# Retention and token-mixing kernel on one core: the q loads of batches 2 and 3 issued from the scalar engine, and 15 instead of 24 zero matmuls at the start

## The chip, the core and the metric

The kernel runs on one core of one Trainium2 chip. The number that counts is the device time of one execution in microseconds, as the median of several executions. Engines are called by the names of the profile: PE is TensorE's matmul, PEld its weight load, DVE is VectorE, ACT is ScalarE, POOL is GpSimd, SP is SyncE. SP computes nothing here: it issues the DMAs.

## The reference: what is computed

Inputs are q, k and v of shape (batch 4, heads 8, sequence 768, head size 64) and three weight matrices, all float32. The first half is a decaying linear attention, written as a recurrence over the sequence:

```
state = gamma[h] * state + outer(k[t], v[t])
y[t]  = q[t] @ state / sqrt(64)
```

The heads of y are laid side by side to x of shape (4, 768, 512). The second half mixes tokens:

```
wq, wk = x @ w_q, x @ w_k
mixed  = (wq @ wk.T / sqrt(64)) @ x
out    = relu(mixed) @ w_out
```

The output has the shape (4, 768, 512) in float32.

## The kernel before, in words

The sequence of a batch is cut into six chunks of 128 tokens, and two chunks make a pair, so there are 12 pairs, numbered p = 0 to 11, three to a batch: pairs 0 to 2 are batch 0, pairs 9 to 11 are batch 3. The recurrence is done chunk by chunk: scores inside a chunk, masked, times v, plus q times the state that the chunks before left. The decay is folded into k by a table (fk, fk2) and into the result by another (gx).

The kernel is written as a list of short tokens, ORDER (lines 18 to 68). Each engine issues its own instructions in the order in which the tokens stand there. A token has a name, a pair, sometimes PSUM banks after "@", and after ":" the engine that does it (A is ACT, V is DVE, P is POOL). These matter here:

- ck, cq, cv cast k, q and v of a pair from their staging buffer to bf16 (function cast, from line 391); trk, trq transpose k and q on PE, ekT, eqT bring the transposed tiles out of PSUM.
- sc makes the scores of a chunk, eat masks them, st adds a chunk to the state in PSUM, es copies the state out (es.5.0:A is the copy for pair 5, chunk 0, on ACT), in and ia make the two parts of y, ex scales it.
- xt, exN, wqk, ew, za, zm, ez, mx, r, pj, eo are the second half. pj is the output projection, and eo copies its result out of PSUM and issues the store (line 770).
- warmup issues matmuls of a zero tile (line 374), fill issues a few more between the first real ones.

Loads. All loads of batches 0 and 1, and the weights, are issued at the start from SP in the order of LOADS (line 77), pair by pair, 512 KB each. Batches 2 and 3 come into the same staging buffers, which batches 0 and 1 have left: a load may go out once the cast that read the buffer is done. In the kernel before these loads are issued from inside cast. After the cast of q of pair p (p below 6) come the two loads of 256 KB for q of pair p+6 (load_pair, lines 204 to 223). After the last cast of k or v of a batch comes one load of 1.5 MB for the whole of k or v two batches on (load, line 202). In what follows k2B, v2B, k3B and v3B are these four loads for batches 2 and 3. q6 to q11 are the q loads of pairs 6 to 11, each in two halves a and b.

Since all these DMAs are issued from SP, they go out in the order of the tokens: q6, q7, k2B, q8, v2B, q9, k3B, q10, q11, v3B, and then the 24 stores. The framework puts in all the waits. It gives each DMA one of eight semaphores, in turn, which the DMA raises when it has landed.

Of the kernel before, what the change touches and what calls it, by code (L numbers as in the profile page):

```python
# [15 lines left out]


ORDER = """
warmup.24 cv.0:A ck.0:V trk.0@4 ekT.0:V cq.0:P fill.3 trq.0@5
eqT.0:V fill.5 sc.0.0@0+1 sc.0.1@2+3 st.0.0 es.0.0:A in.0.1@4 eat.0.0:V  # L20
ia.0.0@5 eat.0.1:V ia.0.1 st.0.1 ck.1:P trk.1@6 cq.1:A es.0.1:A
ekT.1:A ck.2:P ex.0.0:V ex.0.1:V trq.1@2 eqT.1:V fill.1 sc.1.0@0+1
# [7 lines left out]
za.0@4 zm.0 sc.3.1@0+1 ck.4:P WO:A ck.5:P cv.4:P st.3.1  # L30
ez.0:V mx.1@4+5 mx.0@6+2 r.1.1:A r.0.0:A r.0.1:A eat.3.1:V cq.4:V
in.3.1@5 trk.4@6 trq.4@2 r.1.0:V pj.1.1@4 ekT.4:V es.3.1:V eqT.4:A
ia.3.0@6 sc.4.0@0+1 ia.3.1 pj.0.1@2 cq.5:P cv.5:P cq.7:P eo.1.1:A
eo.0.1:A pj.0.0@4 eat.4.0:V ex.3.1:V ex.3.0:V mx.2@5+2 st.4.0 cq.6:P
trk.5@6 r.2.1:V sc.4.1@0+1 trq.5@2 es.4.0:V eqT.5:V r.2.0:A eo.0.0:A
ekT.5:A st.4.1 in.4.0@4 wqk.3@5 in.4.1@6 eat.4.1:V ia.4.0 sc.5.0@2+3
ia.4.1 ew.3:V es.4.1:A sc.5.1@0+1 st.5.0 es.5.0:A pj.2.0@5 eo.2.0:A
ex.4.0:V eat.5.0:V ex.4.1:V pj.2.1@4 in.5.0@5 in.5.1@2 trq.6@6 eo.2.1:A
eqT.6:A pj.1.0@4 ia.5.0 eat.5.1:V ia.5.1 ex.5.1:V ex.5.0:V xt.3@6
eo.1.0:A xt.4@4 exN.4:V wqk.4@2 xt.5@5 ew.4:V exN.5:V exN.3:A  # L40
wqk.5@6 ck.6:P cq.8:A trk.6@4 ew.5:A trq.8@2 zm.1@5 ekT.6:V
eqT.8:V sc.6.1@0+1 trq.7@4 ck.7:P trk.7@6 ez.1:A mx.4@5+2 eat.6.1:V
sc.6.0@0+1 ck.8:P eqT.7:A r.4.0:A ekT.7:V mx.3@4+6 trk.8@5 r.4.1:A
sc.7.1@2+3 r.3.1:A r.3.0:A eat.6.0:V sc.7.0@0+1 pj.4.0@6 ekT.8:A pj.3.0@4
eo.4.0:A eat.7.1:V eat.7.0:V cv.6:P st.6.0 sc.8.1@2+3 sc.8.0@0+1 es.6.0:A
st.6.1 eo.3.0:A ia.6.0@5+6 ia.6.1 cv.8:P cv.7:P in.6.1 es.6.1:A
st.7.0 eat.8.1:V es.7.0:A cq.9:P pj.3.1@4 ex.6.0:V ex.6.1:V in.7.0@5+2
st.7.1 ia.7.0 ia.7.1 eo.3.1:A in.7.1 eat.8.0:V ex.7.0:V es.7.1:A
in.8.0@4+6 st.8.0 ia.8.1 es.8.0:A ia.8.0 in.8.1 ex.7.1:V trq.9@5
ex.8.1:V ex.8.0:V wqk.7@2 xt.7@6 exN.7:V ew.7:V eqT.9:A xt.6@5  # L50
xt.8@4 exN.6:V ck.9:P trk.9@6 wqk.8@2 cq.10:A exN.8:A trq.10@5
ekT.9:V mx.5@4+6 sc.9.1@0+1 ew.8:A sc.9.0@2+3 eqT.10:V ck.10:P trk.10@5
r.5.1:A r.5.0:A eat.9.1:V eat.9.0:V ekT.10:A ck.11:P cq.11:A wqk.6@6
pj.4.1@4 eo.4.1:V sc.10.0@0+1 sc.10.1@2+3 trk.11@5 trq.11@4 ew.6:A pj.5.1@6
ekT.11:A eat.10.1:V eqT.11:V eat.10.0:V zm.2@5 cv.9:P st.9.0 eo.5.1:A
ia.9.0@4+6 ia.9.1 es.9.0:A in.9.1 st.9.1 ez.2:V mx.6@5+2 es.9.1:A
sc.11.1@0+1 r.6.1:A cv.10:P st.10.0 es.10.0:A ex.9.1:V pj.5.0@6 r.6.0:A
st.10.1 eat.11.1:V eo.5.0:A mx.7@5+2 sc.11.0@0+1 ex.9.0:V es.10.1:A r.7.1:A
cv.11:P in.10.0@6+4 in.10.1 ia.10.0 st.11.0 ia.10.1 pj.6.0@2 eat.11.0:V
r.7.0:A ex.10.1:V ex.10.0:V in.11.0@4+5 es.11.0:A in.11.1 ia.11.0 ia.11.1  # L60
ex.11.1:V ex.11.0:V eo.6.0:A pj.7.1@6 xt.10@5 eo.7.1:V wqk.10@2 wqk.9@4
ew.9:V ew.10:A exN.10:A xt.11@6 exN.11:V xt.9@2 exN.9:V wqk.11@4
ew.11:A pj.6.1@5 za.3@4 zm.3 mx.8@6+2 eo.6.1:A ez.3:A r.8.0:A
r.8.1:V pj.7.0@5 pj.8.1@4 mx.9@6+2 eo.7.0:A r.9.0:A r.9.1:V eo.8.1:A
pj.8.0@5 eo.8.0:V pj.9.0@6 mx.10@4+5 eo.9.0:V r.10.1:A pj.9.1@2 mx.11@5+6
eo.9.1:A r.10.0:V pj.10.0@4 eo.10.0:V pj.10.1@2 eo.10.1:V r.11.1:A r.11.0:A
pj.11.0@5 eo.11.0:V pj.11.1@4 eo.11.1:A
""".split()


SPLIT = (0, 1)


BY_PAIR = ("q2", "q3")
# [9 lines left out]
def kernel(  # L84
# [19 lines left out]
    nc = tc.nc  # L104
# [25 lines left out]
    def buf(name, i, shape, dtype):  # L130

        if (name, i) not in made:
            made[name, i] = const(f"{name}{i}", shape, dtype)
        return made[name, i]
# [25 lines left out]
    def copy(e, out, in_):  # L160
        if e == "A":
            nc.scalar.copy(out=out, in_=in_)  # L162
        else:
            ENGINES[e].tensor_copy(out=out, in_=in_)  # L164
# [4 lines left out]
    def split(p):  # L169
        return p // NP in SPLIT  # L170
# [11 lines left out]
    def whole(name, b):  # L182
        return name != "q" and b not in SPLIT

    def raw(name, b):
        if (name, b) not in staged:
            staged[name, b] = buf(name + "_st", b % 2, [H * NCH * D], FP32)
        return staged[name, b]

    def stage(name, b):  # L190

        order = "n h e" if b in SPLIT or f"{name}{b}" in BY_PAIR else "h n e"
        return raw(name, b).rearrange(
            f"p ({order}) -> p n h e", n=NCH if whole(name, b) else NP, h=H
        )

    def load(name, b):
        if whole(name, b):
            n, src = NCH, SRC[name][b].rearrange("h (n p) d -> p (h n) d", p=128)
        else:  # L200
            n, src = NP, SRC[name][b].rearrange("h (n p j) d -> p (h n) (j d)", p=128, j=2)
        nc.sync.dma_start(out=raw(name, b).rearrange("p (m e) -> p m e", m=H * n), in_=src)

    def load_pair(name, p):
        b, n = divmod(p, NP)
        src = SRC[name][b, :, n * 2 * C : (n + 1) * 2 * C, :]
        if whole(name, b):
            for c in range(2):
                nc.sync.dma_start(
                    out=stage(name, b)[:, 2 * n + c],  # L210
                    in_=src[:, c * C : (c + 1) * C, :].rearrange("h p d -> p h d"),
                )
        elif split(p):
            nc.sync.dma_start(  # L214
                out=stage(name, b)[:, n], in_=src.rearrange("h (p j) d -> p h (j d)", j=2)
            )
        else:

            for o in range(2):
                nc.sync.dma_start(  # L220
                    out=stage(name, b)[:, n, o * HP : (o + 1) * HP],
                    in_=src.rearrange("(m o) (p j) d -> o p m (j d)", o=2, j=2)[o],
                )
# [6 lines left out]
    for part in LOADS:  # L230
        if part == "W":
            nc.sync.dma_start(out=wq_stage, in_=moe_w_q.rearrange("(a p) h -> p a h", p=128))  # L232
            nc.sync.dma_start(out=wk_stage, in_=moe_w_k.rearrange("(a p) h -> p a h", p=128))  # L233
        elif part == "WO":
            nc.sync.dma_start(out=wout_stage, in_=moe_w_out.rearrange("(a p) m -> p a m", p=128))  # L235
        elif part[0] in SRC:
            load_pair(part[0], int(part[1:]))
        else:
            load(part[0].lower(), int(part[1:]))
# [8 lines left out]
    def temp(i):  # L248

        return buf("o0_", 2, [DM], FP32)[:, i * 64 : i * 64 + NCH * H]  # L250
# [22 lines left out]
    lq = temp(3).rearrange("p (n j h) -> p n j h", n=NP, j=2)  # L273
# [60 lines left out]
    for t, base in ((cmask2, 0), (cmask2_b, C)):  # L334
        nc.gpsimd.memset(t, 1.0)
        for j in range(2):
# [4 lines left out]
                fill=0.0,  # L341
# [49 lines left out]
    def cast(e, name, p, table):  # L391
        st = pairs[p]
        b, cp = divmod(p, NP)
        t = buf(name + "s", p % N_CAST, [2, H, D], BF16)
        st[name + "s"] = t
        if whole(name, b):
            in_ = stage(name, b)[:, 2 * cp : 2 * cp + 2]
        else:
            in_ = stage(name, b)[:, cp].rearrange("p h (j d) -> p j h d", j=2)
        if table is None:  # L400
            copy(e, t, in_)
        elif split(p):
            ENGINES[e].tensor_tensor(  # L403
                out=t, in0=in_, in1=table.to_broadcast([128, 2, H, D]), op=ALU.mult
            )
        else:

            for j in range(2):
                ENGINES[e].tensor_tensor(  # L409
                    out=t[:, j].rearrange("p (o m) d -> p o m d", o=2),  # L410
                    in0=in_[:, j].rearrange("p (m o) d -> p o m d", o=2),
                    in1=table[:, j]
                    .rearrange("p (m o) -> p o m", o=2)[:, :, :, None]
                    .to_broadcast([128, 2, HP, D]),
                    op=ALU.mult,
                )
        casts[name, b] = casts.get((name, b), 0) + 1

        if b + 2 in SPLIT or f"{name}{b + 2}" in BY_PAIR:
            load_pair(name, p + 2 * NP)  # L420
        elif casts[name, b] == NP and b + 2 < B:
            load(name, b + 2)

    def ck(e, at, p):
        cp = p % NP
        cast(e, "k", p, fk2[:, cp] if split(p) else fk[:, 2 * cp : 2 * cp + 2])

    def cq(e, at, p):
        cast(e, "q", p, None)

    def cv(e, at, p):
        cast(e, "v", p, None)
# [331 lines left out]
    def eo(e, at, p, j):  # L764
# [8 lines left out]
        "ck": ck, "cq": cq, "cv": cv, "trk": trk, "ekT": ekT, "trq": trq, "eqT": eqT, "sc": sc,  # L773
        "eat": eat, "msk": msk, "st": st_, "es": es, "in": in_, "ia": ia, "ex": ex, "xt": xt,
        "exN": exN, "wqk": wqk, "ew": ew, "za": za, "zm": zm, "ez": ez, "mx": mx, "r": r,
        "pj": pj, "eo": eo, "W": W, "WO": WO, "fill": fill, "warmup": warmup,
    }

    for token in ORDER:
        token, _, e = token.partition(":")  # L780
        token, _, at = token.partition("@")
# [33 lines left out]
```

## Time and profile before

| | |
|---|---|
| time, median of 3 | 103.28 us (103.1 to 104.06) |
| span of the profiled execution | 102.8 us |
| PE busy | 87.8 us, 85% |
| PEld busy | 61.1 us, 59% |
| DVE busy | 76.6 us, 75% |
| ACT busy | 60.8 us, 59% |
| POOL busy | 40.2 us, 39% |
| DMA | 26.71 MB, mean 260 GB/s |
| granted TensorE clock | 1.0 over the span |

The profile is of one execution. Its views name an instruction by line, engine, operation and the tiles that it writes and reads. A line of a timeline gives the start and the length in us, then the instruction, then in square brackets the idle time of the engine before it and what ended it. "SPq" marks a DMA issue on SP; its length is the time that the issue took on SP, not the time in which the data moved. A line of waits gives the total, the number and the longest of a kind of wait, in us. A line of windows gives a stretch of the execution, for each engine its busy time in the stretch with the number of instructions, and at its end the granted clock, the busy share of the DMA engines and the GB/s.

### The profile page before, as it was taken

Reading aid. Unit: us, or ns where it says so; the run is one execution under the profiler, and the core shown is the slowest. Engines: PE = TensorE matmul, PEld = TensorE weight load, DVE = VectorE, ACT = ScalarE, POOL = GpSimd, SP = SyncE. Lnnn points to the kernel's source line nnn. Section 1 sums busy time; section 2 is a strip of 40 time slices with the busy share of each in tenths; the row PEclk is TensorE's granted clock in tenths of the full one; section 3 lists DMA queues with packets and bytes.
Section 4 is the critical chain, followed back from the end, with each engine's and each line's share of the span. In section 5 each row is a group of like instructions: output and inputs, shape, how many; then the busy total and the mean of one; then the engine's idle time right before and its main releaser. Section 6 shows DMA issues by size and latency. Waiting matters only on the chain.

```text
span 102.8 us, 3767 instructions
## 1 busy us (share of the span) xinstructions
PE 87.8 (85%) x1607; PEld 61.1 (59%) x1617; DVE 76.6 (75%) x124; ACT 60.8 (59%) x104; POOL 40.2 (39%) x51
## 2 busy tenths in 40 slices
PE   5999668597976989999899789958999999999950
PEld 1347557486864748868776357847665669533410
DVE  5845777989989597995888699855998976248440
ACT  6784664228689638367549454339967825564620
POOL 6843654900024296705980690399055000000000
PEclk9999999999999999999999999999999999999999
DMA  1999999999988999967992699999799932036663
GB/s 25 303 347 347 347 343 245 267 305 367 341 240 255 341 336 303 331 195 204 267 305 59 196 262 326 270 276 293 242 406 403 380 134 105 4 131 233 247 263 145
DMA packets 36320, 26.71 MB, mean 260 GB/s; under 512 B 2000, under 2 KB 32720, under 8 KB 36304
## 3 DMA queue, kind: packets, MB, share of 16 engines
q1 hardware_dynamic: 36304, 26.48, 82.6%
q8 instruction: 12, 0.20, 0.7%
q14 instruction: 4, 0.03, 0.1%
HBM read 20.19 MB, written 6.29 MB: 257 GB/s over the span
## 4 chain that ended last, share of the span: by engine, by line
SPq 34%; PE 32%; issue 12%; POOL 10%; DMA 5%; ACT 2%; DVE 1%; POOLq 0%; ACTq 0%
SPq L214 25%; PE bank_ps L755 11%; POOL ks L409 6%; DMA q_st<-in_q_dram 5%; SPq L220 3%; POOL vs L164 3%; PE duo_ps L755 3%; PE bank_ps L441 2%; SPq L235 2%; PE bank_ps L734 2%; PE bank_ps L598 2%; PE bank_ps L651 2%; SPq L233 2%; PE bank_ps L553 2%; SPq L232 2%
## 5 line engine op out<-in xcount | busy, mean ns | idle before, releaser
L755 PE MATMUL bank_ps<-wout_sb,relu 128*128 128x512 bf16 x72 | 18.9, 380 | 0.6 <-issue 0.3
L162 ACT CAST s_sb<-bank_ps 64x256 bf16<-64x256 f32 (+1 forms) x26 | 9.6, 370 | 14.9 <-PE bank_ps L598 14.8
L509 DVE TENSOR_TENSOR at<-duo_ps,cmask 128x1024 bf16<-128x1024 f32 x12 | 14.5, 1220 | 2.2 <-PE duo_ps L486 2.2
L638 DVE TENSOR_TENSOR xT<-bank_ps,gx 128x512 bf16<-128x512 f32 x22 | 14.4, 685 | 2.3 <-PE bank_ps L571 1.0
L502 DVE TENSOR_TENSOR at<-duo_ps,cmask 128x1024 bf16<-128x1024 f32 x12 | 14.5, 1218 | 2.0 <-PE duo_ps L475 2.0
L409 POOL TENSOR_TENSOR ks<-k_st,fk 128x512 bf16<-128x512 f32 x12 | 12.2, 1048 | 8.0 <-PE bank_ps L651 4.4
L164 POOL CAST vs<-v_st 128x1024 bf16<-128x1024 f32 x10 | 10.2, 1038 | 10.3 <-DMA v_st<-in_v_dram 10.3
L403 POOL TENSOR_TENSOR ks<-k_st,fk 128x1024 bf16<-128x1024 f32 x4 | 7.6, 1903 | 16.0 <-PE bank_ps L708 9.5
L755 PEld LDWEIGHTS <-relu 128*128 128x128 bf16 x96 | 8.2, 98 | 8.9 <-issue 0.6
L162 ACT COPY o<-bank_ps 128x512 f32<-128x512 f32 x14 | 8.2, 586 | 4.4 <-PE bank_ps L755 4.4
L747 ACT ACTIVATE relu<-bank_ps 128x512 bf16<-128x512 f32 x15 | 8.6, 603 | 2.5 <-PE bank_ps L734 1.1
L162 ACT CAST qs<-q_st 128x1024 bf16<-128x1024 f32 x6 | 6.3, 1046 | 3.6 <-DMA q_st<-in_q_dram 3.6
L598 PE MATMUL bank_ps<-vs,ks 64*64 64x64 bf16 (+1 forms) x240 | 7.5, 195 | 1.1 <-POOL vs L164 1.1
L376 PE MATMUL bank_ps<-warm 128*128 128x512 bf16 x24 | 7.0, 465 | 1.2 <-DVE warm L246 1.2
L598 PEld LDWEIGHTS <-ks 64*64 64x64 bf16 (+1 forms) x240 | 6.0, 109 | 3.1 <-issue 1.9
L441 PE MATMUL bank_ps<-identity,ks 128*128 128x128 bf16 x88 | 7.0, 220 | 0.8 <-POOL ks L409 0.6
L164 DVE COPY kT<-bank_ps 128x1024 bf16<-128x1024 bf16 x6 | 4.1, 688 | 4.0 <-PE bank_ps L441 4.0
L441 PEld LDWEIGHTS <-ks 128*128 128x128 bf16 x96 | 5.6, 98 | 2.4 <-POOL ks L409 1.0
L475 PE MATMUL duo_ps<-qT,kT 64*64 64x128 bf16 x192 | 4.6, 219 | 2.9 <-DVE qT L164 1.1
L441 PEld LDWEIGHTS <-qs 128*128 128x128 bf16 x96 | 5.8, 98 | 1.5 <-ACT qs L162 1.2
L164 POOL CAST qs<-q_st 128x1024 bf16<-128x1024 f32 x5 | 5.1, 1039 | 3.0 <-DMA q_st<-in_q_dram 3.0
L651 PEld LDWEIGHTS <-xT 128*128 128x128 bf16 x96 | 5.7, 98 | 0.5 <-issue 0.2
(98 smaller groups left out, 167.4 us busy)
## 6 DMA issues: line engine op xcount, KB each, us to landing
out_dram<-o SPq DMA_DIRECT2D x24, 256.0 KB, 2.8
k_st<-in_k_dram SPq DMA_DIRECT2D x6, 512.0 KB, 6.0
q_st<-in_q_dram SPq DMA_DIRECT2D x6, 512.0 KB, 6.2
v_st<-in_v_dram SPq DMA_DIRECT2D x6, 512.0 KB, 7.0
q_st<-in_q_dram SPq DMA_DIRECT2D x12, 256.0 KB, 4.9
wout_stage<-in_moe_w_out_dram SPq DMA_DIRECT2D x1, 1024.0 KB, 9.6
o<-in_moe_w_q_dram SPq DMA_DIRECT2D x1, 128.0 KB, 6.2
o<-in_moe_w_k_dram SPq DMA_DIRECT2D x1, 128.0 KB, 5.0
```

The costliest lines, as they stand in the source:

```text
L162: nc.scalar.copy(out=out, in_=in_)
L164: ENGINES[e].tensor_copy(out=out, in_=in_)
L214: nc.sync.dma_start(out=stage(name, b)[:, n], in_=src.rearrange("h (p j) d -> p h (j d)", j=2))
L409: ENGINES[e].tensor_tensor(out=t[:, j].rearrange("p (o m) d -> p o m d", o=2), in0=in_[:, j].rearrange("p (m o) d -> p o m d", o=2), in1=t ...
L441: nc.tensor.transpose(ps[:, i, hp, :] if whole(name, p // NP) else slots[:, :, hp, i, :], pairs[p][name + "s"][:, i, 2 * hp : 2 * hp + 2, ...
L502: nc.vector.tensor_tensor(out=t.rearrange("p x (hi j) t -> p (x hi) (j t)", j=2), in0=ps.rearrange("p x (hi j) t -> p (x hi) (j t)", j=2), ...
L509: nc.vector.tensor_tensor(out=t.rearrange("p x hp t -> p (x hp) t"), in0=ps.rearrange("p x hp t -> p (x hp) t"), in1=cmask.rearrange("p o ...
L598: nc.tensor.matmul(out=state_ps[rows(x), m, :], lhsT=st["ks"][ps, slot, 2 * m + x, :], rhs=st["vs"][ps, slot, head(p, m, x), :], start=(n ...
L638: nc.vector.tensor_tensor(out=st["xT", i], in0=st["y", i], in1=table, op=ALU.mult)
L651: nc.tensor.transpose(ps[:, c, a, :], xT(p, a, c), identity)
L747: nc.scalar.activation(out=dst, in_=st["mx"][half], func=ACT.Relu)
L755: nc.tensor.matmul(out=ps, lhsT=st["relu", a // 2][:, a % 2, j], rhs=wout_sb[:, a, :], start=(a == 0), stop=(a == NDM - 1),)
```

## The change

Two things are changed. First, the q loads of batches 2 and 3 are no longer issued from SP by cast. They have tokens of their own, lq.6 to lq.11, which issue the two halves from ACT's DMA queue at a place in ACT's order that ORDER sets. SP then has only k2B, v2B, k3B, v3B and the stores left after the loads of the start. This is to keep the small q loads from standing behind the large k and v loads, and the large ones behind them. Second, 15 zero matmuls instead of 24 stand ahead of the first transposes on PE. They keep PE busy until the first k has come. The rest of ORDER keeps its sequence; some PSUM banks around pairs 6 to 8 are others.

```diff
-warmup.24 cv.0:A ck.0:V trk.0@4 ekT.0:V cq.0:P fill.3 trq.0@5
+warmup.15 cv.0:A ck.0:V trk.0@4 ekT.0:V cq.0:P fill.3 trq.0@5
...
+ia.3.0@6 sc.4.0@0+1 ia.3.1 pj.0.1@2 cq.5:P cv.5:P lq.6:A lq.7:A
+cq.7:P eo.1.1:A eo.0.1:A pj.0.0@4 eat.4.0:V ex.3.1:V ex.3.0:V mx.2@5+2
...
+ia.4.0 sc.5.0@2+3 ia.4.1 ew.3:V es.4.1:A sc.5.1@0+1 st.5.0 lq.8:A
+es.5.0:A pj.2.0@5 eo.2.0:A ex.4.0:V eat.5.0:V ex.4.1:V pj.2.1@4 in.5.0@5
+in.5.1@2 trq.6@6 eo.2.1:A lq.9:A eqT.6:A pj.1.0@4 ia.5.0 eat.5.1:V
+ia.5.1 ex.5.1:V ex.5.0:V xt.3@6 eo.1.0:A xt.4@4 exN.4:V wqk.4@2
+xt.5@5 ew.4:V exN.5:V exN.3:A wqk.5@6 ck.6:P lq.10:A cq.8:A
+trk.6@4 ew.5:A trq.8@5 zm.1@6 ekT.6:V eqT.8:V sc.6.1@0+1 trq.7@4
+ck.7:P trk.7@5 ez.1:A mx.4@6+2 eat.6.1:V sc.6.0@0+1 ck.8:P lq.11:A
+eqT.7:A r.4.0:A ekT.7:V mx.3@4+5 trk.8@6 r.4.1:A sc.7.1@2+3 r.3.1:A
...
-    def load_pair(name, p):
+    def load_pair(name, p, queue=nc.sync):
...
-                nc.sync.dma_start(
+                queue.dma_start(
...
-        if b + 2 in SPLIT or f"{name}{b + 2}" in BY_PAIR:
+        if name == "q":
+            pass
+        elif b + 2 in SPLIT or f"{name}{b + 2}" in BY_PAIR:
             load_pair(name, p + 2 * NP)
         elif casts[name, b] == NP and b + 2 < B:
             load(name, b + 2)
+
+    def lq_(e, at, p):
+
+        load_pair("q", p, nc.scalar)
```

More of the change, by code (lines that the diff above doesn't have):

```diff
@@ L32 @@
 in.3.1@5 trk.4@6 trq.4@2 r.1.0:V pj.1.1@4 ekT.4:V es.3.1:V eqT.4:A
[L33 to L67, printed above, removed]
+ia.3.0@6 sc.4.0@0+1 ia.3.1 pj.0.1@2 cq.5:P cv.5:P lq.6:A lq.7:A
+cq.7:P eo.1.1:A eo.0.1:A pj.0.0@4 eat.4.0:V ex.3.1:V ex.3.0:V mx.2@5+2
+st.4.0 cq.6:P trk.5@6 r.2.1:V sc.4.1@0+1 trq.5@2 es.4.0:V eqT.5:V
@@ new lines @@
+r.2.0:A eo.0.0:A ekT.5:A st.4.1 in.4.0@4 wqk.3@5 in.4.1@6 eat.4.1:V
+ia.4.0 sc.5.0@2+3 ia.4.1 ew.3:V es.4.1:A sc.5.1@0+1 st.5.0 lq.8:A
[5 more added lines that the diff above has]
+ck.7:P trk.7@5 ez.1:A mx.4@6+2 eat.6.1:V sc.6.0@0+1 ck.8:P lq.11:A
@@ new lines @@
+eqT.7:A r.4.0:A ekT.7:V mx.3@4+5 trk.8@6 r.4.1:A sc.7.1@2+3 r.3.1:A
+r.3.0:A eat.6.0:V sc.7.0@0+1 pj.4.0@5 ekT.8:A pj.3.0@4 eo.4.0:A eat.7.1:V
+eat.7.0:V cv.6:P st.6.0 sc.8.1@2+3 sc.8.0@0+1 es.6.0:A st.6.1 eo.3.0:A
+ia.6.0@5+6 ia.6.1 cv.8:P cv.7:P in.6.1 es.6.1:A st.7.0 eat.8.1:V
+es.7.0:A cq.9:P pj.3.1@4 ex.6.0:V ex.6.1:V in.7.0@5+2 st.7.1 ia.7.0
+ia.7.1 eo.3.1:A in.7.1 eat.8.0:V ex.7.0:V es.7.1:A in.8.0@4+6 st.8.0
+ia.8.1 es.8.0:A ia.8.0 in.8.1 ex.7.1:V trq.9@5 ex.8.1:V ex.8.0:V
+wqk.7@2 xt.7@6 exN.7:V ew.7:V eqT.9:A xt.6@5 xt.8@4 exN.6:V
@@ new lines @@
+ck.9:P trk.9@6 wqk.8@2 cq.10:A exN.8:A trq.10@5 ekT.9:V mx.5@4+6
+sc.9.1@0+1 ew.8:A sc.9.0@2+3 eqT.10:V ck.10:P trk.10@5 r.5.1:A r.5.0:A
+eat.9.1:V eat.9.0:V ekT.10:A ck.11:P cq.11:A wqk.6@6 pj.4.1@4 eo.4.1:V
+sc.10.0@0+1 sc.10.1@2+3 trk.11@5 trq.11@4 ew.6:A pj.5.1@6 ekT.11:A eat.10.1:V
+eqT.11:V eat.10.0:V zm.2@5 cv.9:P st.9.0 eo.5.1:A ia.9.0@4+6 ia.9.1
+es.9.0:A in.9.1 st.9.1 ez.2:V mx.6@5+2 es.9.1:A sc.11.1@0+1 r.6.1:A
+cv.10:P st.10.0 es.10.0:A ex.9.1:V pj.5.0@6 r.6.0:A st.10.1 eat.11.1:V
+eo.5.0:A mx.7@5+2 sc.11.0@0+1 ex.9.0:V es.10.1:A r.7.1:A cv.11:P in.10.0@6+4
@@ new lines @@
+in.10.1 ia.10.0 st.11.0 ia.10.1 pj.6.0@2 eat.11.0:V r.7.0:A ex.10.1:V
+ex.10.0:V in.11.0@4+5 es.11.0:A in.11.1 ia.11.0 ia.11.1 ex.11.1:V ex.11.0:V
+eo.6.0:A pj.7.1@6 xt.10@5 eo.7.1:V wqk.10@2 wqk.9@4 ew.9:V ew.10:A
+exN.10:A xt.11@6 exN.11:V xt.9@2 exN.9:V wqk.11@4 ew.11:A pj.6.1@5
+za.3@4 zm.3 mx.8@6+2 eo.6.1:A ez.3:A r.8.0:A r.8.1:V pj.7.0@5
+pj.8.1@4 mx.9@6+2 eo.7.0:A r.9.0:A r.9.1:V eo.8.1:A pj.8.0@5 eo.8.0:V
+pj.9.0@6 mx.10@4+5 eo.9.0:V r.10.1:A pj.9.1@2 mx.11@5+6 eo.9.1:A r.10.0:V
+pj.10.0@4 eo.10.0:V pj.10.1@2 eo.10.1:V r.11.1:A r.11.0:A pj.11.0@5 eo.11.0:V
@@ L68 @@
+pj.11.1@4 eo.11.1:A
 """.split()
@@ L213, in load_pair @@
         elif split(p):
-            nc.sync.dma_start(
+            queue.dma_start(
                 out=stage(name, b)[:, n], in_=src.rearrange("h (p j) d -> p h (j d)", j=2)
@@ L219, in load_pair @@
             for o in range(2):
-                nc.sync.dma_start(
+                queue.dma_start(
                     out=stage(name, b)[:, n, o * HP : (o + 1) * HP],
@@ L775 @@
         "exN": exN, "wqk": wqk, "ew": ew, "za": za, "zm": zm, "ez": ez, "mx": mx, "r": r,
-        "pj": pj, "eo": eo, "W": W, "WO": WO, "fill": fill, "warmup": warmup,
+        "pj": pj, "eo": eo, "W": W, "WO": WO, "fill": fill, "warmup": warmup, "lq": lq_,
     }
```

## The prediction

> **What bounds the kernel now.** I read first the order of time of SP's issues, then the DMA rate by windows, then the waits of the other engines, then ACT and PE around the places where the new tokens stand.
>
> The timeline of SP from 30 us on:
>
> ```profile
> 31.59 1.91 SPq L214 DMA_DIRECT2D v_st<-in_v_dram  x1
> 33.62 3.84 SPq L220 DMA_DIRECT2D q_st<-in_q_dram  x4
> 37.66 1.39 SPq L202 DMA_DIRECT2D k_st<-in_k_dram  x1
> 39.15 7.54 SPq L220 DMA_DIRECT2D q_st<-in_q_dram  x2
> 46.90 0.71 SPq L202 DMA_DIRECT2D v_st<-in_v_dram  x1
> 47.71 9.47 SPq L220 DMA_DIRECT2D q_st<-in_q_dram  x2
> 57.39 0.71 SPq L202 DMA_DIRECT2D k_st<-in_k_dram  x1
> 58.19 7.24 SPq L220 DMA_DIRECT2D q_st<-in_q_dram  x4
> 65.64 1.32 SPq L202 DMA_DIRECT2D v_st<-in_v_dram  x1
> 67.06 6.87 SPq L770 DMA_DIRECT2D out_dram<-o  x1
> ```
>
> The loads of 1.5 MB are issued in 0.7 to 1.4 us, but whatever stands behind one is stuck for 6 to 9 us: the queue takes the next DMA only when the large one is nearly moved. SP is stuck from 37.7 to 74 us. The windows show what that costs the DMA engines: each time the queue has run dry before the next DMA is in it.
>
> ```profile
> 44.00:45.00 1.00, 1.00 (x9) 0.53 (x8) 1.00 (x2) 0.58 (x1) 0.00 (x0) 1.00 1.01 305
> 45.00:46.00 1.00, 1.00 (x18) 0.88 (x16) 1.00 (x2) 0.69 (x2) 0.00 (x0) 1.00 0.35 93
> 53.00:54.00 1.00, 1.00 (x20) 0.71 (x18) 1.00 (x2) 0.80 (x1) 0.64 (x1) 1.00 0.95 288
> 55.00:56.00 1.00, 1.00 (x25) 0.79 (x23) 0.71 (x2) 1.00 (x3) 0.00 (x0) 1.00 0.15 41
> ```
>
> The waits on these loads:
>
> ```profile
> POOL vs L164 <- DMA v_st<-in_v_dram: 10.3, 4, 3.9
> POOL ks L409 <- DMA k_st<-in_k_dram: 3.6, 1, 3.6
> ACT qs L162 <- DMA q_st<-in_q_dram: 3.6, 2, 2.8
> ```
>
> But these are waits of POOL and ACT. PE issues in a fixed order and had other work: comparing each matmul's start with the length of the one before, its gaps of over 0.25 us after 45 us that end on a cast are 0.42 (50.8 us), 0.89 (58.6), 0.33 (60.5), 0.77 (68.0), 0.78 (69.6), and 0.45 at 70.6 behind them: 3.6 us. That is all a faster delivery of batches 2 and 3 can give. PE's busy share from 33 us to 97 us is near 94%.
>
> **What the Trainium skill says.** "DMA: Bandwidth & Descriptors", section "Issuing engines are not separate DMA queues": DMAs from SP and ACT run on the same 16 engines, so a second issuer saves issue time, not transfer time; the trace of before has one issuer only and does not show it. The same page, section "Why a DMA increments its semaphore by 16 and not by 1": two DMAs in flight on one semaphore can't be told apart, so each one in flight needs its own. The trace agrees with what follows: its records name eight semaphores for the DMAs, used strictly in turn; the first eight loads wait for nothing, and from the ninth on (10.80 us) every issue waits on the semaphore that it is about to use, until the DMA eight places earlier has landed. "Perfetto Trace Analysis", section "DMA Instruction — HWDGE (DVE, Sync)": the recorded length of an issue holds the wait for the descriptor generator, which one issuer locks, and its work, not the wait for semaphores. The 6.74 us of the first q8 half against 0.75 for the second are such a wait. "TensorE: Matmul & The Clock Gate", Part 1: after some 3.4 us without work the clock halves and takes as long to come back; the first eight zero matmuls start 0.43 us apart, the later ones 0.215.
>
> **The change, part by part.**
>
> *Warm-up.* The 24 zero matmuls last to 8.12 us. The nine dropped are late ones at 0.215: 1.9 us, so PE is free at 6.2, and k of pair 0, cast by DVE at 5.05 for 1.23, is ready at 6.28. The first transposes can come 1.8 us earlier. But the loads of the start are paced by the DMA engines at some 345 GB/s, and st.4.0 at 38.4 us waits for v of pair 4, cast on POOL behind k of pair 5, which lands at 35.3. Early gains end there: 0 us, bounds -1.5 and 0.
>
> *q off SP.* This takes 12 issues off SP. k2B can go at 33.6 instead of 37.7, and the large loads follow each other. Nothing on PE gains more than the 3.6 us.
>
> *q onto ACT.* The issues behind no large load take 0.45 to 0.75 us on SP; I take 0.65. ACT's queue is in order, so behind lq.6 and lq.7 stands eo.1.1, whose bank pj.0.0 needs on PE: 4 x 0.65, less 1.0 us beside eqT.4's copy, 1.6 us. The other eight issues, 5.2 us, fall partly into idle time of ACT (1.75 us at 43 us, 0.81 at 49.7): 1 us on the path, bounds 0 and 3.
>
> *The added wait.* This decides. I number the DMAs by the program: 21 loads at the start, then k2B, v2B, k3B and v3B (emitted at ck.2, cv.2, ck.5 and cv.5), lq.6 and lq.7 (four), the stores of eo.1.1, eo.0.1 and eo.0.0, and then lq.8. Its first half is the eighth after v3B: it takes v3B's semaphore and must wait, on ACT, until v3B has landed. Nothing in the data asks for that. In the order of before, the DMA eight places earlier was always long landed, since one queue issued all. Now ACT's load is due at 43 us and SP's large one is the last of four.
>
> ```profile
> 43.19 0.74 ACT L162 CAST s_sb<-bank_ps 64x256 bf16<-64x256 f32 x2 [1.75 <-PE bank_ps L598]
> 44.14 0.58 ACT L162 COPY o<-bank_ps 128x512 f32<-128x512 f32 x1 [0.21 <-PE bank_ps L755]
> 44.81 0.39 PE L540 MATMUL bank_ps<-qT,s_sb 128*128 128x128 bf16 x4
> ```
>
> Behind lq.8 on ACT stand es.5.0 and eo.2.0 (the first two lines). PE's in.5.0 (the third) writes the bank that eo.2.0 empties, so PE stops there, and DVE soon after.
>
> When does v3B land? The slices of the page give 9.6 MB moved by 33.4 us. Up to v3B the program moves 10.75 MB (start) + 1.05 (q6, q7) + 4 x 1.57 = 18.1 MB. The 8.5 MB left take 26.6 us at 320 GB/s, between the 313 of the middle of v2B and the 340 with q: 60.0 us. Three gaps between large loads remain, since each is let in only as the last runs dry; with the dips above I take 1.5 us each, bounds 0 and 3. Completion adds 0.5. So v3B lands at 65 us, bounds 61 and 70 (before: 75.5).
>
> Then two issues (1.3), es.5.0 (0.74), eo.2.0 (0.58) and a semaphore: in.5.0 at 67.75 instead of 44.81, +22.9. From there the old course runs, with the 3.6 us of waits gone, since all of k and v is there. PE has idled for some 20 us and starts at half clock: +1.5, bounds 0 and 1.7. Later issues on ACT: +1; the 1.6 at lq.6 vanishes in the wait. Sum: 103.3 + 22.9 - 3.6 + 1.5 + 1 = **125.1**.
>
> **The rivals.**
>
> *A: the two queues don't tie each other* (the order in which semaphores are dealt across engines, or their number, spares ACT). Then 103.3 - 3.6 + 1.6 + 1 - 0.8 (half of the warm-up's bound) = 101.5. For it: the waits above and the dips. Against it: the strict turn of eight.
>
> *B: the tie is to an earlier load.* Across engines the dealing may follow another order than the program's; then a wait falls on k3B, which I expect near 57. 57 + 2.75 - 44.81 = 15, less 3, plus 1.5: 116.
>
> *C: no semaphore, but the descriptor generator.* If SP holds it while it is stuck, ACT's four issues of lq.6 and lq.7 come only between SP's, the last behind v3B's issue at some 54 us; pj.0.0 moves from 36.2 to 55, +18.8, less 3.6, plus 2.5: 121.
>
> **How the numbers follow.** Main case 0.68, A 0.13, B 0.12, C 0.07. The forecast is the main case, 125. Its own spread is v3B's landing, 121 to 130; with B and C the range 108 to 131 leaves out A and tails of the rest, under 2 in 10. Faster needs A with its gain whole: 0.09; within 1% 0.03 (A with dearer issues); slower 0.88.
>
> **What would show it.** Right: ACT idle for some 20 us ahead of the issue of lq.8 and es.5.0, ended as v_st lands near 65 us; PE and DVE near zero from about 50 to 65; k2B issued at about 34; no POOL wait on v_st of any length after it; the start of the first transposes at 6.3 us. Wrong: ACT's DMA issues without idle time before them, or long lengths of these issues themselves (then C), or v3B landing much before 60. If the end of the idle time is the landing of k_st, B holds.

## The result, and the profile after

| | before | after |
|---|---|---|
| median | 103.67 us (103.1 to 104.4) | 110.68 us (109.61 to 111.6) |
| ratio after to before, 95% interval | | 1.0638 (1.0516 to 1.076) |
| span of the profiled execution | 102.8 us | 108.9 us |
| PE busy | 87.8 us | 87.4 us |
| granted TensorE clock, mean | 1.0 | 0.977 |

The kernel is slower by some 7 us, where 21.7 were forecast. PE did the same work in the same busy time; what was added is waiting. (A ratio is taken from the faster executions of each kernel alone, so it need not be the ratio of the medians.) The chain that ended last already names it. In order of time, with start, length and instruction, its middle part after the change is:

```profile
33.57 1.28 SPq L203
...
35.30 17.75 DMA v_st<-in_v_dram
...
54.10 1.02 ACT qT L163
55.16 1.18 PE bank_ps L658 x16
```

A transfer of v stands in the chain for 17.75 us, and what follows its end is a copy of transposed q on ACT (eqT.6) that reads no v at all. So ACT waited on a load that its work does not need, as forecast; but the load landed at 53.05 us, and the place is not the one forecast.

ACT's timeline around it (start, length, instruction, and in brackets the idle time before):

```profile
34.78 3.96 ACTq L221 DMA_DIRECT2D q_st<-in_q_dram  x4
38.83 0.59 ACT L163 COPY o<-bank_ps 128x512 f32<-128x512 f32 x1 [3.13 <-DVE xT L645]
...
43.07 0.37 ACTq L221 DMA_DIRECT2D q_st<-in_q_dram  x1
...
45.47 0.38 ACTq L221 DMA_DIRECT2D q_st<-in_q_dram  x1
45.89 0.75 ACT L163 CAST s_sb<-bank_ps 64x256 bf16<-64x256 f32 x2 [2.08 <-PE bank_ps L605]
46.66 1.30 ACT L163 COPY o<-bank_ps 128x512 f32<-128x512 f32 x2
53.07 0.94 ACTq L221 DMA_DIRECT2D q_st<-in_q_dram  x2
54.10 1.01 ACT L163 COPY qT<-bank_ps 128x1024 bf16<-128x1024 bf16 x1 [6.14 <-issue]
```

In the kernel before, eqT.6 ran at 45.90, right behind its transposes:

```profile
45.90 1.01 ACT L162 COPY qT<-bank_ps 128x1024 bf16<-128x1024 bf16 x1 [0.31 <-PE bank_ps L441]
```

The issues on ACT are lq.6 and lq.7 (34.78), the halves of lq.8 (43.07 and 45.47) and lq.9 (53.07). The cast to s_sb at 45.89, which is es.5.0, and eo.2.0 behind it come only 2.7 us later than before. This is the place where the prediction let ACT stop for 20 us. The long idle time, 6.14 us, is one token group later, ahead of lq.9. "Issue" as its end means that the profile shows nothing on the copy itself that came last; ACT's sequencer stood at the DMA ahead of it.

SP's timeline after the change answers the first view of the prediction:

```profile
33.57 1.28 SPq L203 DMA_DIRECT2D k_st<-in_k_dram  x1
35.30 7.84 SPq L203 DMA_DIRECT2D v_st<-in_v_dram  x1
43.60 7.39 SPq L203 DMA_DIRECT2D k_st<-in_k_dram  x1
51.45 4.56 SPq L203 DMA_DIRECT2D v_st<-in_v_dram  x1
56.11 14.92 SPq L777 DMA_DIRECT2D out_dram<-o  x9
```

The four large loads now follow each other, and k2B goes out at 33.57 instead of 37.66. They land at 45.45, 53.05, 57.75 and 66.35 us. Before, v2B, k3B and v3B landed at 57.43, 65.71 and 75.54. The same four windows as in the prediction (DMA share and GB/s are the last two columns, PE's busy time the second) show that the queue no longer runs dry at these places:

```profile
44.00:45.00 1.00, 1.00 (x65) 0.90 (x66) 0.96 (x2) 0.00 (x0) 0.00 (x0) 1.00 1.09 340
45.00:46.00 1.00, 0.95 (x38) 0.70 (x28) 0.86 (x2) 0.11 (x1) 0.00 (x0) 1.00 1.03 306
53.00:54.00 1.00, 0.00 (x0) 0.00 (x0) 0.00 (x0) 0.00 (x0) 1.00 (x2) 1.00 1.07 325
55.00:56.00 1.00, 0.84 (x15) 0.83 (x15) 0.00 (x0) 0.79 (x3) 1.00 (x2) 1.00 1.12 341
```

The 93 and 41 GB/s of before are 306 and 341 now. One dip is left, from 50 to 52 us, with 193 GB/s. So the change did what it is for. At 53 us, though, PE, DVE and ACT do nothing.

Of the waits after (total, number, longest), these four matter here:

```profile
...
POOL qs L165 <- DMA q_st<-in_q_dram: 9.8, 3, 7.2
ACT qT L163 <- issue: 6.1, 1, 6.1
...
PE bank_ps L658 <- ACT qT L163: 3.9, 1, 3.9
...
POOL vs L165 <- DMA v_st<-in_v_dram: 2.6, 2, 2.2
```

POOL's waits on v at the cast are 2.6 us, where they were 10.3. POOL's wait on q has grown to 9.8 us (3.0 before), since q6 and q7 now land at 43.3 to 46.9 us instead of 39.0 to 41.7, while k2B and v2B are under way from SP. New are ACT's and PE's wait at eqT.6.

On PE three new gaps are left, each with its end:

```profile
39.47 1.02 PE L762 MATMUL bank_ps<-wout_sb,relu 128*128 128x512 bf16 x4 [2.10 <-ACT o L163]
...
49.17 0.62 PE L448 MATMUL bank_ps<-identity,qs 128*128 128x128 bf16 x8 [1.26 <-POOL qs L165]
...
55.16 1.18 PE L658 MATMUL bank_ps<-identity,xT 128*128 128x128 bf16 x16 [3.94 <-ACT qT L163]
```

Counted from start to start, as in the prediction, these are 2.27, 1.43 and 4.10 us. The first is pj.0.0, whose bank eo.1.1 copies out only at 38.83 (35.27 before), behind the issues of lq.6 and lq.7. (ACT's timeline names DVE as the end of the idle time there, but the last of the four issues ends at 38.74, and in e6 below, without these issues on ACT, eo.1.1 runs at 34.79.) The second is trq.6, which waits for late q: POOL casts pair 7 ahead of pair 6, and the last half of q7 lands at 46.94. The third is xt.3 behind eqT.6. After the third the clock is down (windows, the clock is the third column from the right):

```profile
56.00:58.00 2.00, 2.00 (x27) 2.00 (x25) 1.03 (x2) 1.86 (x2) 2.00 (x3) 0.51 1.13 339
58.00:60.00 2.00, 2.00 (x30) 2.00 (x28) 0.91 (x2) 0.29 (x2) 0.79 (x2) 0.64 1.11 346
60.00:62.00 2.00, 2.00 (x38) 1.59 (x36) 1.57 (x3) 0.56 (x2) 2.00 (x3) 1.00 1.12 345
```

2 x 0.49 and 2 x 0.36 make 1.7 us of full-speed work lost, if all of PE's work is bound by its clock. The gaps of before at 50.8, 58.6, 60.5, 68.0, 69.6 and 70.6 us, 3.6 us in all, are gone. The ledger: 2.27 + 1.43 + 4.10 + 1.7 - 3.6 = 5.9 us, and the spans differ by 6.1. The profiled execution of the kernel before took 104.55 us, 0.9 more than the median, so some 1 us of the 7 between the medians is not in this ledger.

**Which DMA waits for which.** The records of the DMAs name the semaphore that each waits for and raises. The eight are dealt in turn; with the first load of the kernel as turn 0, and with the landing times of the trace (us), they read:

```
turn     DMA            engine   landed     waits for the landing of (8 turns back)
21       k2B            SP       45.45      a load of batch 1
22       v2B            SP       53.05      the load of w_out
23 - 26  q6a q6b q7a q7b ACT     43.32 ...  loads of batch 1
27       k3B            SP       57.75      a load of batch 1
28       q8a            ACT      49.91      a load of batch 1
29       q8b            ACT      52.72      k2B   45.45  (issued 45.47)
30       q9a            ACT      58.44      v2B   53.05  (issued 53.07)
31       q9b            ACT      59.16      q6a   43.32
32       v3B            SP       66.35      q6b   45.63
33 - 34  q10a q10b      ACT      63.62 ...  q7a, q7b  46.25, 46.94
35       q11a           ACT      66.99      k3B   57.75  (issued 61.45, no wait)
```

The eight semaphores are dealt strictly in turn over both engines, as the prediction took it. The turns keep each engine's own order, but between the two engines they do not follow the tokens: in the built program v3B, whose token stands ahead of lq.6, has its turn after q9. So v3B is not eight ahead of q8; v2B is eight ahead of q9. What makes the framework interleave the engines in this way is not shown by a trace. The second half of q8 is tied to a large load as well, k2B. This cost little here: k2B landed at 45.45, and the matmuls that es.5.0 behind it needs ran from 45.09 to 45.51.

### The profile page after: what moved, and what is told of

It is laid out like the page before. It is cut to its first block, busy times and chain, and to the rows that moved or that the text cites. A ratio compares the mean times of both kernels' runs of the same rounds, so it can differ in the third digit from the quotient of the medians.

```text
span 108.9 us, 3743 instructions
## 1 busy us (share of the span) xinstructions
PE 87.4 (80%) x1598; PEld 61.3 (56%) x1608; DVE 76.6 (70%) x124; ACT 61.0 (56%) x104; POOL 40.1 (37%) x51
## 4 chain that ended last, share of the span: by engine, by line
PE 44%; SPq 31%; DMA 16%; ACT 3%; issue 2%; ACTq 1%
SPq L215 23%; DMA v_st<-in_v_dram 16%; PE bank_ps L762 12%; PE bank_ps L448 5%; PE bank_ps L658 4%; PE duo_ps L493 3%; PE duo_ps L762 3%; SPq L236 3%; PE bank_ps L741 2%; PE bank_ps L715 2%; PE bank_ps L605 2%; PE bank_ps L560 2%; PE bank_ps L589 2%; SPq L234 2%; SPq L203 2%
## 5 line engine op out<-in xcount | busy, mean ns | idle before, releaser
L658 PE MATMUL bank_ps<-identity,xT 128*128 128x128 bf16 x80 | 6.3, 229 | 4.2 <-ACT qT L163 3.9
L163 ACT COPY qT<-bank_ps 128x1024 bf16<-128x1024 bf16 x4 | 4.0, 1012 | 8.1 <-issue 6.1
L165 DVE COPY x<-bank_ps 128x1024 bf16<-128x1024 bf16 x7 | 4.8, 686 | 4.5 <-PE bank_ps L658 4.5
L448 PE MATMUL bank_ps<-identity,qs 128*128 128x128 bf16 x72 | 5.5, 220 | 1.4 <-POOL qs L165 1.4
```

Source lines behind the costliest of these rows:

```text
L448: nc.tensor.transpose(ps[:, i, hp, :] if whole(name, p // NP) else slots[:, :, hp, i, :], pairs[p][name + "s"][:, i, 2 * hp : 2 * hp + 2, ...
L658: nc.tensor.transpose(ps[:, c, a, :], xT(p, a, c), identity)
```

## The experiments

The theory that was tested: lq.9 waits on ACT for v2B by a shared semaphore, and most of the loss is this wait; the rest is the issues of lq.6 and lq.7 on ACT and late q. Its rivals: the warm-up; DMAs on a second queue as such; late q landings alone. All times are medians. The kernel before was measured again beside them: 103.95 us beside e1 to e4, 104.15 beside e5 to e8, 103.53 beside e9 and e10, 103.22 beside e11. Ratios are to it.

**e1 and e2: the two halves of the change.** The kernel before with

```diff
-warmup.24 cv.0:A ck.0:V
+warmup.15 cv.0:A ck.0:V
```

and the kernel after with the opposite edit.

> The kernel before with 15 zero matmuls instead of 24, nothing else. Theory (the loss is a semaphore wait on ACT's queue, the warm-up does nothing): first transposes at 6.2 us instead of 8.1, the lead gone by st.4.0 near 38 us, 103.2 to 103.8 us. Rival (the warm-up takes part in it, by a colder clock): over 104.5 us and a granted clock under 1.0 early on.

> The q loads on ACT as in the changed kernel, with the 24 zero matmuls of before. Theory: 110.7 us, as the changed kernel within 0.7. Rival (warm-up takes part): 105 to 109 us.

e1 took 104.47 us (100.68 to 106.2) beside 103.95 (102.45 to 107.11): the two overlap wholly, and no difference can be told. Its trace, of an execution of 106.09 us, has the early lead used up by gaps on PE at 29.7 us (1.18) and 33.4 us (1.62). It also has the clock at half from 20.4 to 23.8 us and from 34.1 to 37.5 us, which the rival expected. e2 took 110.62 us, ratio 1.0623 (1.0485 to 1.076), the same as the whole change. Its ACT shows the same wait for v2B:

```profile
52.92 0.94 ACTq L221 DMA_DIRECT2D q_st<-in_q_dram  x2
53.97 1.01 ACT L163 COPY qT<-bank_ps 128x1024 bf16<-128x1024 bf16 x1 [5.31 <-issue]
```

So the loss comes with q on ACT and needs no part of the warm-up. Whether the shorter warm-up has a cost of its own in the clock stays open: of the eleven traces of kernels with 15 zero matmuls (the kernel after, e1, e3 to e11), seven have a stretch at half clock that begins before 35 us, of the two with 24 none. No run separates this from other causes.

**e3: lq.9 moved out of the way.** In the kernel after:

```diff
-in.5.1@2 trq.6@6 eo.2.1:A lq.9:A eqT.6:A ...
+in.5.1@2 trq.6@6 eo.2.1:A eqT.6:A ...
...
-eqT.7:A r.4.0:A ...
+eqT.7:A lq.9:A r.4.0:A ...
```

and in the same way lq.10 behind ekT.8 and lq.11 behind es.7.0.

> The changed kernel with lq.9, lq.10 and lq.11 later in ACT's order (behind eqT.7, ekT.8 and es.7.0). The semaphore that v2B raises is then dealt next to v3B, which SP issues, and lq.9 takes one that q6 has long raised. Theory: eqT.6 follows its transposes at once, PE's 4.1 us gap at 55 us and the half clock after it (some 1.2 us) are gone: 105.4 us (104.5 to 106.5), still slower than before by what lq.6 and lq.7 cost. Rival (the cost is ACT's issuing and the two queues sharing the DMA engines, as many issues as ever): 109.5 to 111 us.

Measured 110.2 us, ratio 1.0576 (1.0465 to 1.0686): a miss. The wait for v2B was gone: eqT.6 ran at 51.28 us, right behind its transposes, and PE had no gap there. But moving the tokens changed the deal. Now q10b waited for q9a (landed at 62.84), and the halves of q11 for two stores, which stood behind v3B on SP and landed at 67.32 and 68.07:

```profile
67.40 1.09 ACTq L221 DMA_DIRECT2D q_st<-in_q_dram  x2
68.53 0.59 ACT L163 COPY o<-bank_ps 128x512 f32<-128x512 f32 x1 [2.68 <-DMA out_dram<-o]
```

PE waited 2.04 us for what stood behind it. And this run had a longer stretch at half clock, after a PE gap of 2.91 us at 39.6:

```profile
40.00:42.00 2.00, 2.00 (x29) 1.29 (x28) 0.93 (x2) 1.01 (x3) 0.00 (x0) 0.72 1.11 339
42.00:44.00 2.00, 2.00 (x31) 1.44 (x30) 0.35 (x1) 1.10 (x2) 0.00 (x0) 0.50 1.14 345
44.00:46.00 2.00, 2.00 (x33) 1.94 (x34) 1.82 (x2) 0.73 (x2) 0.00 (x0) 0.50 1.09 333
46.00:48.00 2.00, 2.00 (x72) 1.80 (x73) 0.56 (x1) 0.00 (x0) 1.76 (x2) 0.57 1.12 344
```

By the same reckoning as above this is up to 3.4 us of full-speed work lost. So e3 took away one tie and made others; it neither confirms nor refutes the theory.

**e4: the same wait at an earlier token.** In the kernel after:

```diff
-... st.5.0 lq.8:A
+... st.5.0 lq.8:A lq.9:A
 es.5.0:A pj.2.0@5 eo.2.0:A ...
```

with lq.9 taken out of its old place. This leaves the deal as it is: lq.9 still waits for v2B, but now es.5.0 and eo.2.0 stand behind it, the tokens that the prediction named.

> The changed kernel with lq.9 moved ahead of es.5.0, three ACT instructions earlier; the semaphores are dealt as before the move. Theory: ACT stands from 45.9 to 53.1 us until v2B has landed, now with es.5.0, the two copies and eqT.6 all behind it: 112.5 to 114 us. Rival (issuing and sharing): no difference, 110.7 us.

Measured 113.16 us, ratio 1.0797 (1.0646 to 1.0948), in the range that the theory expected. The interval overlaps that of the kernel after, so the time alone does not decide; the trace shows the wait where the theory puts it:

```profile
44.26 9.27 ACTq L221 DMA_DIRECT2D q_st<-in_q_dram  x3
53.58 0.74 ACT L163 CAST s_sb<-bank_ps 64x256 bf16<-64x256 f32 x2 [9.05 <-DMA q_st<-in_q_dram]
```

```profile
54.98 0.58 PE L547 MATMUL bank_ps<-qT,s_sb 128*128 128x128 bf16 x4 [6.92 <-ACT o L163]
```

The first two lines are ACT's: one group of three issues, of which the last two waited until v2B had landed at 52.58, and es.5.0 at once behind it. The third is PE's in.5.0, 7 us idle for eo.2.0. The chain ACT queue, eo.2.0, in.5.0 of the prediction is therefore right as a mechanism; in the kernel after it is only not the place where the semaphore falls.

**e5: lq.9 to lq.11 at places where no deal ties them to a large load.** In the kernel after:

```diff
-in.5.1@2 trq.6@6 eo.2.1:A lq.9:A eqT.6:A ...
+in.5.1@2 trq.6@6 eo.2.1:A eqT.6:A ...
...
-xt.5@5 ew.4:V exN.5:V exN.3:A wqk.5@6 ck.6:P lq.10:A cq.8:A
+xt.5@5 ew.4:V exN.5:V exN.3:A wqk.5@6 ck.6:P cq.8:A lq.9:A
```

with lq.10 behind ez.1 and lq.11 behind r.3.0. Here the turns come out so that q9 waits for the halves of q6, q10 for those of q7, and q11 for q8b and q9a, all landed by then.

> The changed kernel with lq.9 behind cq.8, lq.10 behind ez.1 and lq.11 behind r.3.0. In this order none of the last six q loads takes a semaphore of a large load or of a store; lq.6 to lq.8 stay as they were. Theory (tie of lq.9 to v2B): eqT.6 waits only for its transposes, the 4.1 us gap of PE is gone, and no new tie comes in its place as in the run before: 105.5 to 107.5 us, the rest being lq.6 and lq.7 and some half clock. Rival (issuing and sharing): 109.5 to 111 us.

Measured 105.55 us, ratio 1.0242 (1.0174 to 1.031). Against e2 and the kernel after this is a test of the theory: of the 7 us, 4 to 5 go when lq.9 no longer waits for v2B, with the same DMAs on the same queues, though at later places. What is left shows at lq.6 and lq.7. ACT, then PE, then the clock:

```profile
35.62 4.08 ACTq L221 DMA_DIRECT2D q_st<-in_q_dram  x4
39.79 0.58 ACT L163 COPY o<-bank_ps 128x512 f32<-128x512 f32 x1 [3.24 <-DVE xT L645]
```

```profile
40.42 1.86 PE L762 MATMUL bank_ps<-wout_sb,relu 128*128 128x512 bf16 x4 [2.22 <-ACT o L163]
```

```profile
40.00:42.00 2.00, 1.58 (x4) 0.40 (x3) 0.00 (x0) 0.86 (x2) 0.03 (x1) 0.61 1.12 336
42.00:44.00 2.00, 2.00 (x29) 1.31 (x28) 1.03 (x2) 1.07 (x2) 0.00 (x0) 0.53 1.15 343
```

**e6: q6 and q7 back on SP, ahead of k2B; the others on ACT where the change puts them.** In the kernel after:

```diff
-ia.3.0@6 sc.4.0@0+1 ia.3.1 pj.0.1@2 cq.5:P cv.5:P lq.6:A lq.7:A
+ia.3.0@6 sc.4.0@0+1 ia.3.1 pj.0.1@2 cq.5:P cv.5:P
...
         if name == "q":
-            pass
+            if p < 2:
+                load_pair("q", p + 2 * NP)
```

The turns shift with it. Now q9 and the first half of q10 wait for q6 and q7, the second half of q10 for k2B (landed at 47.92, ahead of its issue at 48.59), and q11 for q8.

> The changed kernel with q6 and q7 issued from SP ahead of k2B, as in the kernel before; lq.8 to lq.11 stay on ACT at their places. The dealing shifts by itself so that lq.8 and lq.9 take semaphores of q5, v5, q6 and q7. Theory (tie, plus ACT blocked at lq.6 and lq.7): both costs are gone, and of the 3.6 us of PE gaps that the late k and v loads cost before, most is won: 100.5 to 102.5 us. Rival (any q on ACT costs by issuing and sharing): 105 to 108 us.

Measured 102.45 us (100.37 to 104.39) beside 104.15, ratio 0.9851 (0.9768 to 0.9934): faster than both kernels, by some 1.5% against the kernel before. On SP the small loads that are needed first go ahead of the large ones, as in the kernel before:

```profile
33.66 3.97 SPq L221 DMA_DIRECT2D q_st<-in_q_dram  x4
37.84 1.76 SPq L203 DMA_DIRECT2D k_st<-in_k_dram  x1
40.05 5.46 SPq L203 DMA_DIRECT2D v_st<-in_v_dram  x1
```

q6 and q7 landed at 40.2 to 42.4 us, and eo.1.1 ran at 34.79. This run is also the control that e5 is not: lq.9 stands at the place that it has in the kernel after, ahead of eqT.6, but its turns are others. v2B landed at 55.83, and ACT did not wait for it:

```profile
45.14 1.22 ACTq L221 DMA_DIRECT2D q_st<-in_q_dram  x2
46.46 1.01 ACT L163 COPY qT<-bank_ps 128x1024 bf16<-128x1024 bf16 x1 [0.74 <-DVE at L510]
```

Gaps of 0.92, 0.74 and 1.30 us were left on PE, the last at eqT.7 behind lq.11, whose second half took 1.55 us to issue:

```profile
52.88 1.96 ACTq L221 DMA_DIRECT2D q_st<-in_q_dram  x2
54.95 1.01 ACT L163 COPY qT<-bank_ps 128x1024 bf16<-128x1024 bf16 x1 [1.71 <-PE duo_ps L494]
```

**e7 and e8: how much of this is the order on SP alone.** e7 issues everything from SP with tokens of its own, in the order q6, q7, q8, k2B, v2B, q9, k3B, q10, q11, v3B (q8 ahead of k2B; before it was behind). e8 has q6 to q8 on SP in this way, and lq.9 to lq.11 on ACT at the places of e3. Both have 15 zero matmuls.

The loads are taken out of cast:

```diff
-sc.1.1@2+3 eat.1.0:V cq.2:A trk.2@4 ...
+sc.1.1@2+3 eat.1.0:V cq.2:A lq.8 lk.2 trk.2@4 ...
...
     def lq_(e, at, p):
...
-        load_pair("q", p, nc.scalar)
+        load_pair("q", p, nc.scalar if e == "A" else nc.sync)
+
+    def lk_(e, at, b):
+        load("k", b)
+
+    def lv_(e, at, b):
+        load("v", b)
```

> All loads on SP, 15 zero matmuls, in the order q6, q7, q8, k2B, v2B, q9, k3B, q10, q11, v3B: q8 is put ahead of k2B, nothing is on ACT. Theory (SP's order of before costs 3.6 us of PE gaps by the late v2B): v2B lands some 3 us earlier than 57.4, k2B one later: 102.3 to 103.3 us. If ACT's queue is what wins in the run with q6 and q7 on SP, this stays behind that by 1 us or more.

> q6, q7 and q8 on SP ahead of k2B; SP then has k2B, v2B, k3B, v3B and the stores; lq.9 behind eqT.7, lq.10 behind ekT.8, lq.11 behind es.7.0 on ACT, none tied to a large load that is still under way except lq.11 to k3B, landed by then. Theory: as with q6 and q7 on SP, k2B one us later: 100.5 to 103 us. Rival (issuing and sharing): above 104 us.

e7 took 103.18 us, ratio 0.9929 (0.9876 to 0.9982); e8 102.97 us, ratio 0.996 (0.9921 to 0.9999). The intervals of e6 and e7 overlap, so these runs do not tell whether the gain of e6 needs the second queue, or only that less stands behind the large loads.

**e9 to e11: what is left at lq.6 and lq.7.** e9 is e5 with

```diff
-... cq.5:P cv.5:P lq.6:A lq.7:A
-cq.7:P eo.1.1:A eo.0.1:A pj.0.0@4 ...
+... cq.5:P cv.5:P
+cq.7:P eo.1.1:A eo.0.1:A lq.6:A lq.7:A pj.0.0@4 ...
```

> The kernel of the run that put lq.9 to lq.11 at places without a slow tie (105.55 us), with lq.6 and lq.7 moved from ahead of eo.1.1 to behind eo.0.1 in ACT's order. Theory (what is left there is the four issues of lq.6 and lq.7 standing ahead of eo.1.1 on ACT, which pj.0.0 on PE waits for): the PE gap of 2.38 us at 40.4 goes, relu 2.0 and eo.0.0 stand behind the issues instead, which costs at most 1 us, q6 and q7 are issued 1 us later; 103.3 to 104.6 us. Rival (what is left is the late landing of q6 and q7, since the two queues share the engines, whatever stands behind the issues): the gap moves to trq.6 near 47 us and grows; 105.2 to 106.5 us.

It took 105.99 us, ratio 1.0373 (1.0286 to 1.0461). The edit put lq.7 behind the cast of pair 7 as well, so that this cast read the old q of pair 1 and did not wait for the new one. With that wait left out, its time does not answer the question. e11 mends that, with cq.7 behind lq.7.

> The kernel with lq.9 to lq.11 at places without a slow tie (105.55 us), with lq.6 and lq.7 behind eo.0.1 in ACT's order, and the cast of q of pair 7 behind them in the program (in the run before this one it stood ahead of lq.7, so that it read the old q of pair 1). Theory (the four issues hold ACT for some 4 us wherever they stand[...]; what stands behind them pays): no gap ahead of pj.0.0, but relu 2.0 and eo.0.0 late, a PE gap of 1.5 to 2.0 us ahead of in.4.0 near 43 us, and a later q6: 104.8 to 106.0 us. Rival (only what pj.0.0 waits for counts, the tokens behind have slack): 102.8 to 104.0 us, no PE gap of over 0.5 us between 36 and 48 us.

Measured 107.37 us, ratio 1.0479 (1.0412 to 1.0546): slower than both expected. PE in this run:

```profile
43.14 0.38 PE L547 MATMUL bank_ps<-qT,s_sb 128*128 128x128 bf16 x4 [2.11 <-ACT o L163]
...
50.80 0.62 PE L448 MATMUL bank_ps<-identity,qs 128*128 128x128 bf16 x8 [2.82 <-POOL qs L165]
```

The first is the gap that the theory named: the four issues took 4.12 us here too, and now eo.0.0 and in.4.0 stood behind them. The second is the rival's: q7's second half landed at 48.57 us, POOL cast pair 7 and then pair 6, and trq.6 was late. Both hold, then: where lq.6 and lq.7 stand early, the copies behind them are late, and where they stand late, q is. The way out was e6, which takes them off ACT and issues them ahead of k2B.

e10 is e6 with one token moved:

```diff
-ck.7:P trk.7@5 ez.1:A mx.4@6+2 eat.6.1:V sc.6.0@0+1 ck.8:P lq.11:A
+ck.7:P trk.7@5 ez.1:A mx.4@6+2 eat.6.1:V sc.6.0@0+1 ck.8:P
...
-r.3.0:A eat.6.0:V ...
+r.3.0:A lq.11:A eat.6.0:V ...
```

> The kernel with q6 and q7 on SP (102.45 us), with lq.11 moved from ahead of eqT.7 to behind relu 3.0 in ACT's order. Theory (the gap of 1.30 us at 56.0 us on PE is eqT.7 behind the held issue of lq.11): the gap goes, 101.0 to 101.9 us. Rival (the gap would only move, since q11 or another load is late in turn, or the end is set elsewhere): 102.2 to 103 us.

Measured 101.91 us beside 103.53, ratio 0.9906 (0.9852 to 0.9961). eqT.7 ran at 54.57 with 0.55 us of idle time ahead of it, and the gap of 1.30 us on PE is gone. Its interval overlaps that of e6, so a gain over e6 is not shown; one over the kernel before, of some 1%, is.

## Why the prediction was right or wrong

The direction and the kind of cause were right: a semaphore that no data asks for made ACT wait for a large load of SP's, and PE waited for the copy behind it. The size was three times too large.

- **The step that failed** is in "The added wait": "I number the DMAs by the program". With that order v3B was eight ahead of q8, and ACT stood at lq.8 until 65 us. In the built program the two engines' DMAs are interleaved in another order, in which v2B is eight ahead of q9. The same sum with this one term replaced: lq.9 goes at v2B's landing, 53.05, plus two issues, 0.94, and a step of 0.1, so eqT.6 starts at 54.10 instead of 45.90, +8.2; less 3.6, plus 1.7 for the clock, is +6.3, against 6.1 between the spans and 7.0 between the medians. This sum was made after the fact. Rival B had just this reason (the dealing follows another order), but with k3B at 57 us as the load, and stood at 116 us (its terms add up to 116.8). It should have been given more weight: the trace of before has one issuer, so it could say how many semaphores there are and that they go in turn, but not in what order two engines are dealt.
- **v3B's landing** was put at 65 us and came at 66.35. This is luck in good part: of the 4.5 us for three gaps between the large loads one dip is left (193 GB/s from 50 to 52 us), and the DMA engines moved q8 to q10 ahead of v3B's end as well, which the forecast held back until v3B had landed. These are six halves of 256 KB, 1.57 MB, which take 4.9 us at the forecast's 320 GB/s. The two errors cancel. **k2B** was put at 33.6 to 34 and went at 33.57.
- **The 3.6 us of waits that faster delivery gives back** are gone from PE's list as forecast.
- **The clock** was put at +1.5, and was about 1.7, but for a gap of 4 us on PE and not for one of 20.
- **The warm-up** at 0: the first transposes start at 6.34 us, as forecast, and e2 shows that the loss does not need it. Whether it is 0 is not shown, as said at e1.
- **lq.6 and lq.7** were put at 1.6 us that vanish in the wait. The issues took 3.96 us, not 2.6, since the last was held for 2.38; PE waited 2.27 us for the copy behind them and 1.43 for late q. (The 0.45 to 0.75 us that the prediction read for one issue leave out 1.64 and 1.31 us, which the first half of q6 and the second half of q9 took on SP before.) In the kernel after, these 3.7 us lie ahead of the wait for v2B, which is fixed by the landing, and so the lateness of ACT is part of the 8.2 and not on top of it. In e5 the wait at lq.6 and lq.7 and the clock are what is left: 2.4 + 1.7 - 3.6 = 0.5, and 1.2 between the spans. By the ratio e5 is 2.4% slower than the kernel before, some 2.5 us, so up to 2 us of it are not accounted for. e5's trace also has half clock from 13.2 to 16.6 us, which this sum does not count.
- **Rival A** forecast 101.5 without the tie. Without the tie alone (e5) it was 105.55, as A had only 1.6 us for lq.6 and lq.7 and nothing for the clock. With these off ACT too, 102.45 (e6).
- **Rival C**, that SP holds the descriptor generator while it is stuck, is refuted: SP's issues of v2B and k3B were stuck from 35.30 to 43.14 and from 43.60 to 50.99 us, and ACT's issues at 35.80 and 45.47, inside these stretches, took 0.52 and 0.38 us. (The 6 to 9 us for which the prediction saw SP stuck behind a large load are lines that join two or four issues; single ones took 5.59 to 8.12 us.) What does hold an issue is open, also for the 6.74 us of the first half of q8 before, which the prediction called a wait for the generator: the trace gives one length for an issue and does not split it.

## What to carry to other kernels

When DMAs are moved to a second engine's queue, find out for each which DMA stands eight turns before it in the built program's dealing of semaphores, and when that one lands; what stands behind the DMA on the new engine waits until then. Small loads that are needed soon go ahead of the large ones on the queue that has no other work, and only loads with time to spare go on an engine that computes. After moving a token, look at the deal again, since every later turn can shift (e3).

## What was not expected of the hardware

- An issue on ACT can be held although ACT's queue has no large load in it: the last of the four issues of lq.6 and lq.7 took 2.38 us in the kernel after, 2.75 in e3 and 2.04 in e11, where the first took 0.41 to 0.42. No run isolated what held it.
- The clock did not follow PE's gaps by their length alone. The Trainium skill ("TensorE: Matmul & The Clock Gate", Part 1) has the clock halve after an idle window of some 3.4 us, and has these windows run on freely, without a reset when a kernel starts. Here the gap of 4.10 us of the kernel after was followed by 0.51 and 0.64. But gaps of 2.38 us (e5) and 2.91 us (e3) were followed by half clock as well, and those of 2.27 us (after, at 39.5 us) and 2.98 us (e11, at 50.8 us) were not.
- The times of the changes agree with free windows: in these traces the stretches of full and of half clock between changes are whole multiples of 3.41 us, such as 51.20, 3.41 and 47.79 us in the kernel after. Counted off in steps of 3.41 us from the changes, the gap of e5 lies inside one window, which ended at 40.46 us as the clock halved. The gap of the kernel after at 39.5 us is cut in two by a window's end at 38.96, and that of e11 by one at 48.92. The windows before half clock were not idle, though: PE was busy for 1.19 us in that of e5, and for 1.77 us in one of e9 (40.77 to 44.18), while one of the kernel after with 1.66 us (35.55 to 38.96) was not followed by half clock. How little work halves the clock stays open.
- The half clock of e3 lasted for 6.83 us with PE busy throughout, twice as long as the 3.41 us in e5 and in the kernel after.
